# A decode block on one core: w_down loaded with seven following rows per partition, the MLP's inner units in steps of seven

## The chip, the cores and the metric

The kernel runs on one core of one Trainium2 chip. The metric is the device time of one execution in microseconds, lower is better. The core has five engines with a queue each: PE (TensorE, matmuls; PEld are its weight loads), DVE (VectorE), ACT (ScalarE), POOL (GpSimd) and SP (SyncE), which here issues the loads. Sixteen DMA engines move the data.

## The reference, cut to what matters

Four tokens (B = 4, one position each, D = 512) go through two layers, both with the same weights and the same cache: attention over a cache of 4,096 positions with 32 query heads and 8 key/value heads of 128, then an MLP with 1,792 inner units. All inputs are bf16.

```python
x = x + A(layernorm(x), k_cache, v_cache, wq, wo)
x = x + B(layernorm(x), w_gate, w_up, w_down)
x = x + A(layernorm(x), k_cache, v_cache, wq, wo)
x = x + B(layernorm(x), w_gate, w_up, w_down)

def B(x, w_gate, w_up, w_down):      # w_gate, w_up: 512 x 1792; w_down: 1792 x 512
    return (sigmoid(x @ w_gate) * (x @ w_up)) @ w_down
```

The sum over the 1,792 inner units of the last product may be taken in any order, if w_gate's and w_up's columns and w_down's rows are taken in the same one.

## The kernel before

**Data.** Keys and values come in loads of 1 MB (one token, one head: 4,096 x 128 bf16) into 12 slots of the on-chip memory (SBUF, 128 partitions); once the last query projection is done, w_q's place serves as four more. Each partition gets 32 following rows, 8,192 bytes in one run. Part of the cache is kept from layer 1 for layer 2 (KEPT). The weights are loaded once and stay: w_q, w_gate and w_up with two following rows per partition, so that a run is as long as two rows; w_o in runs of 1,024 bytes.

**Order.** It is written out by hand. LOADS is the order of the loads: k and v are cache loads, o, g, u, d pieces of the weights; g, u and d stand behind the first 30 loads. `pump` (L340) issues them on SP, in that order, one after another, and stops where no slot is free; a cache load waits on SP until the slot's last reader on PE is done. PROGRAM is the order of the compute steps on PE, DVE, ACT and POOL, one letter per step; a dot is one step of a token's pass from layer 1 to layer 2. Every engine works through its queue in order, and semaphores keep them in step.

**Attention**, for 32 pairs of heads: k is turned by DVE (L983); scores on PE (L1000; four groups of PSUM partitions side by side, 512 columns each, every second element of the keys); row maximum on DVE (L1018), spread over the partitions by PE (L1023); exponential on ACT (L1043); turned back on PE (L1065), copied by ACT (L1117); times the values on PE (L1163, the values as 128x128 weights, four columns streamed); w_o (L1214) and the addition to x on DVE (L1228).

**The MLP of layer 1** is done per token, in four passes (`pass_steps`, L945) spread over layer 1 and the start of layer 2. In a pass the token's normalised x is the weight of a matmul (one column) and w_gate is streamed: `gate_row` (L795) and `up_row` (L820) cut the 1,792 inner units into seven blocks of 256 columns; block f goes to the group of partitions 32*(f % 4), and blocks f and f + 4 share a matmul of 512 columns. So for each of the four parts of D there are four matmuls side by side (three of 512 columns, one of 256), 16 for gate and 16 for up in a pass. The result lies in four rows, partitions 0, 32, 64 and 96 of 512 columns. ACT takes the tanh that stands for the sigmoid (L815), DVE multiplies (L840). `h_turn` (L847) makes columns of it: four matmuls with 128 of the row's columns as weights and `strips`, four columns of the identity that lie 32 elements apart, as what is streamed. `down` (L916, matmuls L922) uses w_down's rows as weights, 56 matmuls with one column each. Then `ln_a`, `ln_b`, `q_row` (L867, matmuls L873: as gate_row, but with w_q in adjacent columns) and `q_turn` (L905) make the queries of layer 2. When the last pass has its queries, `yield_wq` gives w_q's place to the cache loads.

**The MLP of layer 2** is done for all four tokens at the end, behind the last attention: `gate` (L732, matmuls L737) and `up_half` (L764, matmuls L771) use 128 columns of w_gate or w_up as weights and stream four columns, 56 matmuls each; the last product (L1421) has the hidden units as weights and streams w_down, 56 matmuls of 128 columns.

**The order of the inner units before** comes from w_down's load (wparts, L328): block k of 256 rows gives each partition two following rows, a run of 2,048 bytes. Unit e + 2p of the block is then partition p of column e. So `gate` and `up_half` take every second column of w_gate and w_up as weights, and `h_turn` every second column of the row:

```python
"wd": lambda n: (wd_sb[:, 8 * n:min(8 * n + 8, KF), :].rearrange("p (k e) n -> p k e n", e=2),
                 B_w_down[8 * n * P:min(8 * n + 8, KF) * P, :].rearrange("(k p e) n -> p k e n", p=P, e=2)),
```

with KF = 14 blocks of 128 units, KW = 7 and P = 128. The first of the two loads is 1,024 KB, the second 768 KB.

Of the kernel before, what the change touches and what calls it, by code (L numbers as in the profile page):

```python
# [145 lines left out]
def bass_interleave_layers__gqa_block_cached__glu_gated_glu__decode_kernel(  # L146
# [17 lines left out]
    P = 128  # L164
# [3 lines left out]
    KF = F // P  # L168
# [20 lines left out]
    def sbt(shape, dtype, name):  # L189
        cnt[0] += 1  # L190
        return es.enter_context(nc.sbuf_tensor(f"{name}_{cnt[0]}", list(shape), dtype))

    def pst(name):
        return es.enter_context(nc.psum_tensor(name, [P, 512], dt.float32))
# [5 lines left out]
    wg_sb = sbt([P, KD, F], dt.bfloat16, "wg")  # L200
    wu_sb = sbt([P, KD, F], dt.bfloat16, "wu")
    wd_sb = sbt([P, KF, D], dt.bfloat16, "wd")
# [53 lines left out]
    row_sb = t_bf.rearrange("p (h d) -> p h d", h=2)  # L256
# [19 lines left out]
    M_ps = [pst("M_ps0"), pst("M_ps1")]  # L276
# [36 lines left out]
    def two_rows(sb, n):  # L313
        return sb[:, 2 * n:2 * n + 2, :].rearrange("p e n -> p (e n)")

    def row_pairs(w, n):
        return w[2 * n * P:2 * (n + 1) * P, :].rearrange("(p e) n -> p (e n)", e=2)

    def cols(c):
        return bass.ds(c // 2 * 2 * P + c % 2, P, step=2)  # L320

    KW = KF // 2
# [2 lines left out]
                         A_wo[n * REP * P:(n + 1) * REP * P, :].rearrange("(h p) n -> p h n", p=P)),  # L325
        "wg": lambda n: (two_rows(wg_sb, n), row_pairs(B_w_gate, n)),
        "wu": lambda n: (two_rows(wu_sb, n), row_pairs(B_w_up, n)),
        "wd": lambda n: (wd_sb[:, 8 * n:min(8 * n + 8, KF), :].rearrange("p (k e) n -> p k e n", e=2),  # L328
                         B_w_down[8 * n * P:min(8 * n + 8, KF) * P, :].rearrange("(k p e) n -> p k e n", p=P, e=2)),
    }  # L330
    assert KF == 14
    wkeys = {"wg": ["wg0", "wg1"], "wu": ["wu0", "wu1"], "wd": ["wd0", "wd1"]}
# [36 lines left out]
    def dve(fn, reads=(), writes=()):  # L369
        return S.inst("dve", fn, reads=reads, writes=writes)  # L370

    def act(fn, reads=(), writes=()):
        return S.inst("act", fn, reads=reads, writes=writes)
# [34 lines left out]
    for k in range(KD):  # L408
# [3 lines left out]
                lhsT=x_io[0:Bn, cols(k)],  # L412
                rhs=ident_bf[0:Bn, 0:Bn],
# [62 lines left out]
    def bc(ap2, n, nb):  # L476
        return ap2.unsqueeze(1).broadcast_to([P, n, nb])
# [254 lines left out]
    def gate(fc0, fc1):  # L732
        fns = []
        for fc in range(fc0, fc1):
            for k in range(KD):
                fns.append(
                    (lambda fc, k: lambda e: e.matmul(  # L737
                        M_ps[0][:, 64 + fc * Bn:64 + (fc + 1) * Bn],
                        lhsT=wg_sb[:, k, bass.ds(fc // 2 * 2 * P + fc % 2, P, step=2)],
                        rhs=xc_bf[:, k, 0:Bn],  # L740
                        start=(k == 0),
                        stop=(k == KD - 1),
                    ))(fc, k)
                )
        if fc0 == 0:
            S.group("pe", fns, reads=["xcb"] + wkeys["wg"], writes=["M0"])
            return
        S.last_write["M0"] = S.group("pe", fns, reads=["xcb"] + wkeys["wg"])
        dve(
            lambda e: e.tensor_tensor(  # L750
                gs_sb.rearrange("p (k b) -> p k b", k=KF),
                M_ps[0][:, 64:64 + KF * Bn].rearrange("p (k b) -> p k b", k=KF),
                bc(rs, KF, Bn),
                ALU.mult,
            ),
            reads=["M0", "rs"],
            writes=["ra"],
        )
        act(
            lambda e: e.activation(t_sb, gs_sb, ACTF.Tanh),  # L760
            writes=["ra"],
        )

    def up_half(h):  # L764
        M, mk = ((M_ps[1], "M1"), (O_ps[1], "O1"))[h]
        f0 = KW * h
        fns = []
        for fc in range(f0, f0 + KW):
            for k in range(KD):
                fns.append(  # L770
                    (lambda fc, k: lambda e: e.matmul(  # L771
                        M[:, 64 + fc * Bn:64 + (fc + 1) * Bn],
                        lhsT=wu_sb[:, k, bass.ds(fc // 2 * 2 * P + fc % 2, P, step=2)],
                        rhs=xc_bf[:, k, 0:Bn],
                        start=(k == 0),
                        stop=(k == KD - 1),
                    ))(fc, k)
                )
        S.group("pe", fns, reads=["xcb"] + wkeys["wu"], writes=[mk])
        dve(  # L780
            lambda e: e.scalar_tensor_tensor(
                out=hT_bf[:, f0:f0 + KW, :],
                in0=t_sb.rearrange("p (k b) -> p k b", k=KF)[:, f0:f0 + KW, :],
                scalar=1.0,
                in1=M[:, 64 + f0 * Bn:64 + (f0 + KW) * Bn].rearrange("p (k b) -> p k b", k=KW),
                op0=ALU.add,
                op1=ALU.mult,
            ),
            reads=["ra", mk],
            writes=[("rc", "rd")[h]],  # L790
        )

    strips = ident_bf.rearrange("p (s w) -> p s w", s=4)[:, :, 0]

    def gate_row(part):  # L795
        fns = []
        wv = wg_sb.rearrange("p k (f d) -> p k f d", d=2 * P)
        for k in range(2 * part, 2 * part + 2):
            for st in range(4):
                nt = (KW - st + 3) // 4  # L800
                fns.append(
                    (lambda k, st, nt: lambda e: e.matmul(
                        M_ps[0][32 * st:32 * st + 1, 0:nt * 2 * P],
                        lhsT=xc_bf[:, k, 0:1],
                        rhs=wv[:, k, bass.ds(st, nt, step=4), :],
                        start=(k == 0),
                        stop=(k == KD - 1),
                    ))(k, st, nt)
                )
        if part == 0:  # L810
            S.group("pe", fns, reads=["xcb"] + wkeys["wg"], writes=["M0"])
            return
        S.last_write["M0"] = S.group("pe", fns, reads=["xcb"] + wkeys["wg"])
        act(
            lambda e: e.activation(t_row[:, :], M_ps[0][:, :], ACTF.Tanh, scale=rs[:, 0:1]),  # L815
            reads=["rs", "M0"],
            writes=ROW,
        )

    def up_row(part):  # L820
        fns = []
        wv = wu_sb.rearrange("p k (f d) -> p k f d", d=2 * P)
        for k in range(2 * part, 2 * part + 2):
            for st in range(4):
                nt = (KW - st + 3) // 4
                fns.append(
                    (lambda k, st, nt: lambda e: e.matmul(  # L827
                        M_ps[1][32 * st:32 * st + 1, 0:nt * 2 * P],
                        lhsT=xc_bf[:, k, 0:1],
                        rhs=wv[:, k, bass.ds(st, nt, step=4), :],  # L830
                        start=(k == 0),
                        stop=(k == KD - 1),
                    ))(k, st, nt)
                )
        if part == 0:
            S.group("pe", fns, reads=["xcb"] + wkeys["wu"], writes=["M1"])
            return
        S.last_write["M1"] = S.group("pe", fns, reads=["xcb"] + wkeys["wu"])
        dve(
            lambda e: e.scalar_tensor_tensor(  # L840
                out=row_sb[:, 0, :], in0=t_row[:, :], scalar=1.0, in1=M_ps[1][:, :], op0=ALU.add, op1=ALU.mult
            ),
            reads=["rc", "rd", "rb", "M1"],
            writes=["ra"],
        )

    def h_turn():  # L847
        fns = []
        for t in range(2):
            for e_ in range(2):  # L850
                fns.append(
                    (lambda t, e_: lambda e: e.matmul(
                        M_ps[0][:, bass.ds(8 * t + e_, 4, step=2)],
                        lhsT=row_sb[:, 0, bass.ds(2 * P * t + e_, P, step=2)],
                        rhs=strips,
                        start=True,
                        stop=True,
                    ))(t, e_)
                )
        S.group("pe", fns, reads=["ra"] + IDENT, writes=["M0"])  # L860
        dve(
            lambda e: e.tensor_copy(hT_bf[:, :, 0], M_ps[0][:, 0:KF]),
            reads=["M0"],
            writes=["rc", "rd"],
        )
# [520 lines left out]
    for c in range(KD):  # L1386
        for e_ in range(2):
# [3 lines left out]
                    lhsT=xT[:, c // 2 * 2 + e_, :],  # L1391
                    rhs=ident_w[:, P // 2 * (c % 2):P // 2 * (c % 2 + 1)],
# [19 lines left out]
        writes=["rowk"],  # L1412
    )
    up_half(0)
    up_half(1)
    for part in range(2):
        fns = []
        for k in range(KW * part, KW * part + KW):
            for c in range(KD):
# [3 lines left out]
                        lhsT=hT_bf[:, k, :],  # L1423
                        rhs=wd_sb[:, k, c * P:(c + 1) * P],
# [70 lines left out]
```

## Time and profile before

| | |
|---|---|
| median of 3 runs | 313.84 us (313.71 to 313.90) |
| the profiled execution's own time | 316.34 us |
| its span (first to last instruction) | 314.50 us |
| PE, PEld busy | 227.9 us (72%), 146.8 us (47%) |
| DVE, ACT, POOL busy | 176.3 us (56%), 104.5 us (33%), 40.4 us (13%) |
| read from memory | 119.80 MB, 381 GB/s over the span |
| mean granted TensorE clock | 0.74 |

The profile is one execution; its times are in microseconds from the span's start. A busy time counts an instruction from start to end; matmuls overlap, so the busy time of a group is the time covered, and the mean of one can be far longer than their spacing. The 40 slices of the page are 7.9 us each; a digit is the busy share in tenths. The table of stretches has the busy time and number of instructions of PE, PEld, DVE, ACT and POOL in a stretch, then the granted clock, the share of the DMA engines and what they moved. The chain that ended last goes back from the last instruction, at each step to what released it; it is read here in order of time. For a line or tile there are the minimum, median and maximum duration in ns, and the times of the first and last start.

### The profile page before, as it was taken

Reading aid. Unit: us, or ns where it says so; the run is one execution under the profiler, and the core shown is the slowest. Engines: PE = TensorE matmul, PEld = TensorE weight load, DVE = VectorE, ACT = ScalarE, POOL = GpSimd, SP = SyncE. Lnnn points to the kernel's source line nnn. Section 1 sums busy time; section 2 is a strip of 40 time slices with the busy share of each in tenths; the row PEclk is TensorE's granted clock in tenths of the full one; section 3 lists DMA queues with packets and bytes.
Section 4 is the critical chain, followed back from the end, with each engine's and each line's share of the span. In section 5 each row is a group of like instructions: output and inputs, shape, how many; then the busy total and the mean of one; then the engine's idle time right before and its main releaser. Section 6 shows DMA issues by size and latency. Waiting matters only on the chain.

```text
span 314.5 us, 10670 instructions
## 1 busy us (share of the span) xinstructions
PE 227.9 (72%) x4562; PEld 146.8 (47%) x4562; DVE 176.3 (56%) x399; ACT 104.5 (33%) x347; POOL 40.4 (13%) x205
## 2 busy tenths in 40 slices
PE   1233355425969879987789898977777869799966
PEld 1221043413455355746446847254555543455865
DVE  6267625067324568484942675864675777932243
ACT  2002202600213365343325442434334201556420
POOL 0011111001000214111113011020121011121000
PEclk9999999999999999576855557555555575755555
DMA  7999999999999999999999999999999998999910
GB/s 294 419 397 394 410 404 409 402 420 420 400 416 419 373 394 420 424 418 418 420 391 390 417 349 424 425 419 418 418 418 387 412 373 315 380 426 423 414 51 5
DMA packets 20790, 120.49 MB, mean 383 GB/s; under 512 B 1924, under 2 KB 6024, under 8 KB 7688
## 3 DMA queue, kind: packets, MB, share of 16 engines
q1 hardware_dynamic: 20720, 119.81, 94.1%
q8 instruction: 36, 0.59, 0.7%
q14 instruction: 10, 0.08, 0.1%
q10 hardware_dynamic: 24, 0.01, 0.0%
HBM read 119.80 MB, written 0.00 MB: 381 GB/s over the span
## 4 chain that ended last, share of the span: by engine, by line
PE 36%; DMA 34%; DVE 10%; SPq 9%; ACT 6%; issue 4%; POOL 1%; DVEq 0%; ACTq 0%; POOLq 0%
DMA slot<-in_A_v_cache_dram 17%; DMA slot<-in_A_k_cache_dram 13%; PE O_ps L1163 10%; PE S_ps L1000 10%; SPq L366 7%; DVE slot L983 6%; PE PT L1065 4%; DMA wq<-in_A_v_cache_dram 4%; ACT pT L1117 4%; PE O_ps L1214 3%; PE M_ps L873 2%; PE M_ps L922 1%; DVE small L1018 1%; ACT pe L1043 1%; SPq L346 1%
## 5 line engine op out<-in xcount | busy, mean ns | idle before, releaser
L983 DVE STREAM_TRANSPOSE slot<-slot 128x2048 f32<-128x2048 f32 (+1 forms) x55 | 104.6, 1911 | 18.3 <-DMA slot<-in_A_k_cache_dram 18.2
L1117 ACT ACTIVATE pT<-PT 32x128 bf16<-32x128 f32 x236 | 63.1, 267 | 69.2 <-PE PT L1065 33.3
L1000 PE MATMUL S_ps<-slot,qz 128*16 128x512 bf16 x512 | 59.5, 586 | 25.4 <-DVE slot L983 13.2
L1163 PE MATMUL O_ps<-pT,slot 128*128 128x4 bf16 x1696 | 54.8, 166 | 20.0 <-ACT pT L1117 9.9
L1163 PEld LDWEIGHTS O_ps<-pT,slot 128*128 128x128 bf16 x1696 | 51.1, 104 | 34.8 <-ACT pT L1117 13.1
L1043 ACT ACTIVATE pe<-S_ps,small 128x512 bf16<-128x512 f32 x32 | 22.0, 687 | 68.8 <-DVE small L1032 39.1
L1018 DVE TENSOR_REDUCE small<-S_ps 128x1 bf16<-128x512 f32 x32 | 22.0, 689 | 38.2 <-PE S_ps L1000 33.9
L724 POOL COPY qz<-qs 32x32 bf16<-32x32 bf16 x128 | 26.0, 203 | 128.2 <-PE S_ps L1000 87.0
L1065 PE MATMUL PT<-ident_bf,pe 128*128 128x64 bf16 (+1 forms) x288 | 27.7, 236 | 7.8 <-ACT pe L1043 7.2
L1065 PEld LDWEIGHTS PT<-ident_bf,pe 128*128 128x128 bf16 (+1 forms) x288 | 20.4, 124 | 21.6 <-ACT pe L1043 11.4
L1000 PEld LDWEIGHTS S_ps<-slot,qz 128*16 128x16 bf16 x512 | 10.3, 99 | 40.1 <-DVE slot L983 15.1
L1214 PE MATMUL O_ps<-oT,wo 128*128 128x1 bf16 (+1 forms) x640 | 20.3, 165 | 3.7 <-issue 1.8
L1214 PEld LDWEIGHTS O_ps<-oT,wo 128*128 128x128 bf16 x640 | 18.7, 104 | 6.1 <-issue 2.8
L1076 POOL CAST small<-small 128x1 bf16<-128x1 f32 x32 | 6.0, 186 | 94.7 <-ACT pe L1043 67.7
L1194 DVE TENSOR_TENSOR oT<-O_ps,small 128x8 bf16<-128x8 f32 (+1 forms) x32 | 5.3, 165 | 22.3 <-PE O_ps L1163 15.3
L1032 DVE CUSTOM_DVE_ANT_0 MS<-MS,small 128x64 f32<-128x64 f32 x32 | 9.1, 285 | 10.4 <-PE MS L1023 7.4
L873 PE MATMUL M_ps<-wq,small 128*1 128x512 bf16 x128 | 14.6, 609 | 0.0
L1023 PE MATMUL MS<-valid_p,small 128*128 128x64 bf16 x32 | 7.2, 225 | 6.0 <-DVE small L1018 5.9
L1228 DVE TENSOR_TENSOR small<-small,O_ps 128x4 f32<-128x4 f32 (+1 forms) x21 | 3.1, 150 | 13.1 <-PE O_ps L1214 12.9
L888 ACT ACTIVATE t_row<-M_ps,small 128x512 bf16<-128x512 f32 x4 | 2.7, 687 | 23.0 <-DVE small L1032 11.9
L1023 PEld LDWEIGHTS MS<-valid_p,small 128*128 128x128 bf16 x32 | 3.5, 109 | 13.5 <-DVE small L1018 11.7
L827 PE MATMUL M_ps<-wu,small 128*1 128x512 bf16 (+1 forms) x64 | 8.7, 543 | 0.0
(117 smaller groups left out, 182.9 us busy)
## 6 DMA issues: line engine op xcount, KB each, us to landing
slot<-in_A_v_cache_dram SPq DMA_DIRECT2D x49, 1024.0 KB, 12.0
slot<-in_A_k_cache_dram SPq DMA_DIRECT2D x45, 1024.0 KB, 12.0
wq<-in_A_v_cache_dram SPq DMA_DIRECT2D x6, 1024.0 KB, 12.7
wq<-in_A_wq_dram SPq DMA_DIRECT2D x2, 2048.0 KB, 10.1
wo<-in_A_wo_dram SPq DMA_DIRECT2D x8, 512.0 KB, 16.7
wg<-in_B_w_gate_dram SPq DMA_DIRECT2D x2, 896.0 KB, 17.9
wu<-in_B_w_up_dram SPq DMA_DIRECT2D x2, 896.0 KB, 21.3
wd<-in_B_w_down_dram SPq DMA_DIRECT2D x1, 1024.0 KB, 24.1
```

The costliest lines, as they stand in the source:

```text
L366: "sp", (lambda dst, frm: lambda e: e.dma_start(dst, frm))(dst, frm), sem, writes=[key], deps=deps
L724: (lambda a, ps: lambda e: e.tensor_copy(qz_sb[ps, :, :, a, :], qs_sb[b][ps, :, u * REP:(u + 2) * REP].rearrange("p t (u r) -> p u t r", r ...
L873: (lambda k, st: lambda e: e.matmul(M_ps[h][32 * st:32 * st + 1, :], lhsT=xc_bf[:, k, 0:1], rhs=wv[:, k, h, :, st, :], start=(k == 0), sto ...
L983: dve(lambda e: e.transpose(kf, kf), writes=[f"s{st}"])
L1000: (lambda t, b2, e_, c, r0, ul: lambda e: e.matmul(S_ps[p][r0:r0 + 4 * REP, :], lhsT=qz_sb[:, ul, t, :, :].rearrange("p a r -> p (a r)"), ...
L1018: dve(lambda e: e.tensor_reduce(rm_bf, S_ps[p][:, :], AX.X, ALU.max), reads=[f"S{p}"], writes=["rmb"])
L1023: lambda e: e.matmul(MS[:, 0:16 * REP], lhsT=rm_bf.broadcast_to([P, P]), rhs=valid_p[:, :], start=True, stop=True),
L1043: lambda e: e.activation(pe_sb.rearrange("p j m -> p (j m)"), S_ps[p][:, :], ACTF.Exp, bias=nm_sb, scale=exp_scale, accum_out=sm_sb,),
L1065: (lambda q0, q1, c0, m0, m1, a0, a1: lambda e: e.matmul(PT[q0:q1, c0:c0 + 16 * (a1 - a0)], lhsT=pe_flat[:, m0:m1], rhs=valid_bf[:, :, 4 * ...
L1117: (lambda dst, frm: lambda e: e.activation(dst, frm, ACTF.Copy))(dst, frm),
L1163: (lambda n, x, c, j: lambda e: e.matmul(bank[:, ul * REP:(ul + 1) * REP], lhsT=vv[:, x * JG + c * 4 + j, :], rhs=pT[:, x % 2, j, x // 2, ...
L1214: (lambda c, r: lambda e: e.matmul(out_w[:, c * nb:(c + 1) * nb], lhsT=wo_sb[:, us[0] * REP + r, cols(c)], rhs=oT_sb[:, us[0] * REP + r, c ...
```

## The change

w_down is loaded in two equal parts of 896 rows, seven following rows per partition, 7,168 bytes in one run (128 runs per part for 512 and 384 of 2,048 bytes). Inner unit 896h + 7p + j is now partition p of column 7h + j. So the weights of `gate` and `up_half` are 128 columns of w_gate and w_up in steps of seven (14 bytes), and the streamed operands of `gate_row` and `up_row` are, for each of seven values of j, 2 x 128 columns in steps of seven instead of 256 adjacent ones. The row then holds the units in the order of the partitions, and `h_turn` takes 128 adjacent columns as weights; two of its matmuls stream three columns instead of four, and the results are written adjacent.

```diff
-        "wd": lambda n: (wd_sb[:, 8 * n:min(8 * n + 8, KF), :].rearrange("p (k e) n -> p k e n", e=2),
-                         B_w_down[8 * n * P:min(8 * n + 8, KF) * P, :].rearrange("(k p e) n -> p k e n", p=P, e=2)),
+        "wd": lambda n: (wd_sb[:, KW * n:KW * n + KW, :].rearrange("p k n -> p (k n)"),
+                         B_w_down[KW * P * n:KW * P * (n + 1), :].rearrange("(p k) n -> p (k n)", p=P)),
...
@@ gate (L737); up_half (L771) likewise with wu_sb
-                        lhsT=wg_sb[:, k, bass.ds(fc // 2 * 2 * P + fc % 2, P, step=2)],
+                        lhsT=wg_sb[:, k, bass.ds(fc // KW * KW * P + fc % KW, P, step=KW)],
...
@@ gate_row (L797, L802); up_row likewise with wu_sb
-        wv = wg_sb.rearrange("p k (f d) -> p k f d", d=2 * P)
+        wv = wg_sb.rearrange("p k (h q j) -> p k j h q", h=2, j=KW)
...
-                        rhs=wv[:, k, bass.ds(st, nt, step=4), :],
+                        rhs=wv[:, k, bass.ds(st, nt, step=4), :, :],
...
@@ h_turn (L852)
-                        M_ps[0][:, bass.ds(8 * t + e_, 4, step=2)],
-                        lhsT=row_sb[:, 0, bass.ds(2 * P * t + e_, P, step=2)],
-                        rhs=strips,
+                        M_ps[0][:, KW * e_ + 4 * t:KW * e_ + 4 * t + 4 - t],
+                        lhsT=row_sb[:, 0, P * (2 * t + e_):P * (2 * t + e_ + 1)],
+                        rhs=strips[:, 0:4 - t],
```

More of the change, by code (lines that the diff above doesn't have):

```diff
@@ L772, in up_half @@
                         M[:, 64 + fc * Bn:64 + (fc + 1) * Bn],
-                        lhsT=wu_sb[:, k, bass.ds(fc // 2 * 2 * P + fc % 2, P, step=2)],
+                        lhsT=wu_sb[:, k, bass.ds(fc // KW * KW * P + fc % KW, P, step=KW)],
                         rhs=xc_bf[:, k, 0:Bn],
@@ L821, in up_row @@
         fns = []
-        wv = wu_sb.rearrange("p k (f d) -> p k f d", d=2 * P)
+        wv = wu_sb.rearrange("p k (h q j) -> p k j h q", h=2, j=KW)
         for k in range(2 * part, 2 * part + 2):
@@ L829, in up_row @@
                         lhsT=xc_bf[:, k, 0:1],
-                        rhs=wv[:, k, bass.ds(st, nt, step=4), :],
+                        rhs=wv[:, k, bass.ds(st, nt, step=4), :, :],
                         start=(k == 0),
```

## The prediction

> **What bounds the kernel now.** I first read the strip of 40 slices on the profile's page (7.9 us each).
>
> ```profile
> PE   1233355425969879987789898977777869799966
> DMA  7999999999999999999999999999999998999910
> GB/s 294 419 397 394 410 404 409 402 420 420 400 416 419 373 394 420 424 418 418 420 391 390 417 349 424 425 419 418 418 418 387 412 373 315 380 426 423 414 51 5
> ```
>
> The DMA engines are busy from the first slice to about 300 us; after that the transfers are over and 12 us of a tail are left. So two things set the end: how much DMA time is lost before 300 us, and how long the tail is. The second view is the chain that ended last, in order of time (start, length, what). First the tail:
>
> ```profile
> 307.03 0.30 PE M_ps L737 x8
> 307.39 1.27 PE M_ps L737 x48
> 308.66 0.75 PE M_ps L771 x28
> 309.41 0.75 PE O_ps L771 x28
> 310.16 1.62 PE S_ps L1421 x56
> 311.88 0.35 DVE slot L1434
> ```
>
> PE runs here without a break, from the gate (L737) through up (L771) to down (L1421): a nanosecond more on one of its instructions is a nanosecond at the end. Each of the 56 + 56 gate and up matmuls loads 128x128 weights and streams four columns. They follow each other every 1.27 us / 48 = 26.5 ns, so their weight loads set the pace. For the four per-token MLP passes, the chain again and the table of stretches (PE, PEld, DVE, ACT, POOL, clock, DMA share, GB/s):
>
> ```profile
> 85.77 1.83 PE M_ps L827 x4
> 87.70 0.69 DVE t_row L840
> ...
> 104.00:106.00 2.00, 1.20 (x28) 0.56 (x20) 1.67 (x3) 0.00 (x0) 0.81 (x4) 1.00 0.97 356
> 106.00:108.00 2.00, 1.86 (x32) 0.82 (x29) 0.81 (x4) 1.15 (x3) 0.22 (x2) 1.00 0.91 356
> 108.00:110.00 2.00, 2.00 (x36) 1.02 (x35) 0.34 (x1) 1.47 (x7) 0.48 (x3) 1.00 0.95 373
> ```
>
> Pass 1 lies on the chain: from 66.6 to 128.2 us it holds PE, DVE, ACT and POOL work and no transfer. Behind the pass, at 104 to 110 us, the DMA falls from the 420 GB/s that it reaches at 116 to 160 us to 356: SP waits there for PE to give back slots. A delay of PE in pass 1 is therefore lost DMA time.
>
> **The change part by part.**
>
> 1. The loads of w_down. The instruction lists differ on SP only in these two issues: 128x3584 elements each (7,168 bytes in one run per partition) for 128x4x1024 and 128x3x1024 (2,048-byte runs). The trace's packet records add up to 4.94 us of the 16 engines for the 896 packets of 2,048 bytes, and to 8.87 us for the 512 of 7,168 bytes of w_gate and w_up; 256 such would be 4.43. So up to 0.5 us of DMA time goes away, at about 82 to 89 us. I count it as nothing: 15 us later the queue runs low because slots come late, not because bytes are slow, and a DMA that is 0.5 us ahead waits 0.5 us longer there. Were that stall not there, it would be -0.5. The two issues hold SP's queue for 10.18 us (63.48 to 73.65); the issues of w_gate take 0.42 each, so 9.3 us of SP are freed. The loads behind them stand in the same queue behind a DMA share of 1.02, and SP next waits for PE (83.8 to 94.5): 0.
>
> 2. The turn of the row (L852), 16 matmuls in all: weights adjacent instead of every second column, and two of four read three columns for four. They are spaced by 27 ns as contiguous ones are: 0. DVE, ACT and POOL have the same instructions as before.
>
> 3. The steps of seven. The moving operand of the row passes (L802, L827), so far runs of 256 adjacent columns, and the weights of the tail (L737, L771), so far every second column, are now read 14 bytes apart. No instruction on PE of before reads so, and this price decides all. The nearest rows:
>
> ```profile
> 71.39 0.85 PE O_ps L1214 x32
> 93.58 0.85 PE O_ps L1163 x32
> ...
> L737 PE MATMUL M_ps<-small,wg x56: 166/166/186, 307.0 to 308.5; 128*128 128x4 bf16 x56
> L905 PE MATMUL M_ps<-ident_bf,t_row x32: 167/168/188, 100.3 to 267.5; 128*128 128x4 bf16 x32
> L852 PE MATMUL M_ps<-ident_bf,t_row x16: 168/168/189, 90.4 to 255.7; 128*128 128x4 bf16 x16
> ```
>
> L1214's weights are every second column, L1163's adjacent: both 26.6 ns apart, so a step of 4 bytes is free (L1000 streams with that step as well, 16 in 1.81 to 1.91 us, as L873 does adjacent ones). L905 and L852 stream four columns that lie 64 bytes apart, and last 168 ns where four adjacent ones last 166 at the clock of 0.5 (and 164 at 1.0). That is 2 ns over three further columns, **0.67 ns for each column that lies apart** (1.33 at the full clock). So the step of 14 bytes costs between 0 and 0.67 ns a column at the clock of 0.5 that holds in most of the passes and in the tail. I take 0.67: a step of seven passes over six columns of seven, which is nearer to L905's reads, that use one column of 32, than to L1214's, that use every second. It rests on a difference of 2 ns, which is why the other end keeps a large chance.
>
> The Trainium skill speaks on both sides. "SBUF — State Buffer", Specifications, says that a read needs at least two hits in a 16-byte line for full bandwidth; seven bf16 elements apart there is hardly more than one. By it seven of eight columns would pay, and the sum below would be 0.6 us less.
>
> *Tail.* L873's 128 matmuls (32 groups of four, side by side) are busy 14.6 us: 0.456 us a group, 0.89 ns a column. 0.67 more is a ratio of 1.75. The weight loads are paced by columns too (L1163 and L1214: 128 in 26.6 ns, whatever the four or one columns streamed behind), so I give them the same ratio, and 26.5 ns becomes 46.4: 112 x 19.9 = **+2.2 us**, all of it on the chain. Bounds 0 and 3.0 (a doubling). L1421 reads w_down as before.
>
> *Pass 1.* Gate and up are four groups each, 512 columns at the longest: 4 x 512 x 0.67 = 1.37 us each. Gate ends at 85.2, and the next on PE (L1023) waits until 85.5 for DVE (L1018): 0.3 hidden. Up is on the chain. 2.4 us reach the release of slots. What is queued behind on PE is the exponentials' transposes and scores, and SP waits for these. The dip at 104 to 110 us becomes deeper by most of it: **+2.0**, bounds 0.5 and 2.4.
>
> *Passes 2 to 4.* 2.7 us each again. Pass 2 (134.5 to 137.8) is followed by idle times of PE of 0.54, 0.68 and 0.52, the last for a DMA at 142.4, and at 147.7 by 12 us of the chain on a transfer: absorbed. Pass 3 is followed by 0.66 idle for a DMA at 189.8, then by chain work on PE up to 225, over which the DMA is never dry: mostly absorbed. Pass 4 is followed by 0.85 (DMA, 254.8) and 1.80 (DVE behind a DMA, 259.6): 2.65 of 2.7, but its up runs partly at the full clock, where a column pays 1.33, +0.7. I take **+0.6** for all three, bounds 0 and 3.
>
> Sum: 2.2 + 2.0 + 0.6 = +4.8. The profiled execution (316.34 us, span 314.50) would come to 321.1. The runs without profile have a median of 313.84, 2.5 less; the difference carries over, **318.6 us**. With all low or all high bounds of this case (tail 1.4 to 3.0) it is 315.7 to 322.2.
>
> **The rivals.**
>
> *A, not slower: the step of seven is free.* Place: the read of weights and columns; price 0 a column. For it: the step of two costs nothing (26.6 against 26.6 ns), and 14 bytes is much nearer to 4 than to 64; 2 ns of L905 is little. Against: these are the only rows with wide steps, L905 and L852 agree, and at the clock of 1.0 the gap is 4 ns. Then only the DMA's gain is left, 0 to 0.5 us: 313.3 to 313.8, and I would say 313.7. It decides when the price is under about 0.15 ns a column: the tail then costs under 0.5 us, pass 1 is within what its 0.3 us of idle time and the DMA's gain cover. "SBUF — State Buffer", Door 1, says in the box on lines also that one may stride freely by 8 bf16 elements, which this step keeps to; the trace has no row for that.
>
> *B, far slower: the four streams hinder each other,* as four columns or four parts of a weight load are then read from many places at once. If a load of 128 columns went at one column per 0.89 ns, it would take 114 ns: the tail alone + 112 x 87 = 9.8 us (323.6); groups of four times 0.456 us make each pass 11 us longer, and with pass 1 alone it is 334 or more. For it: these loads do go four times faster than one column per 0.89 ns, so parts of them are read side by side. Against: L1000's four streams with their step of two show no loss.
>
> *C: only one of the two reads pays.* Tail alone +2.2 (316.0), passes alone +2.6 (316.4). For it: weights and moving columns are read by separate instructions that overlap (PE and PEld). Against: both are paced by columns.
>
> That the change does not do what it says is out: the two issues and the operand steps are in the instruction lists.
>
> **How the numbers follow.** Forecast case 0.48; A 0.40; B 0.07; C 0.05. This kernel's runs (313.71 to 313.90) can tell apart about 0.2%, 0.6 us. Of A, 0.32 is within that and 0.08 is faster by more (the 0.5 us saved plus transfers that fall better). Faster 0.08, same 0.32, slower 0.60. The range goes from 313.2, A with nearly all its gain, to 322.2, the upper bound of the forecast; B and a part of A's fast end are left out. The forecast's own range is 315.7 to 322.2.
>
> **What would show it.** In the tail, L737's 48 matmuls: 2.2 us for 1.27 if right, 1.27 in A, 5 and more in B. A group of four in L802 and L827: 0.80 us for 0.456. At 104 to 110 us, a DMA share well under 0.91. The issues of w_down at about 0.43 us each and 256 packets of 7,168 bytes more. The forecast is wrong if the tail keeps its length from 307.0 to 311.9, or if the passes are longer and the DMA nevertheless ends at the same time.

## The result and the profile after

The changed kernel takes **324.67 us** (median of 5 runs, 324.07 to 325.28) against 313.78 for the kernel before (5 runs, 313.19 to 313.90): a ratio of 1.0352, 95% interval 1.0334 to 1.0369, or +10.9 us. The forecast was +4.8, with a range up to 322.2: the direction was right, the size forecast was less than half of the measured one. The profiled execution of after took 324.99 us, its span is 323.2, the mean granted clock 0.69.

The strip of 40 slices of after (8.1 us each):

```profile
DMA  7999999999999899999999999999998989999700
GB/s 293 423 396 395 410 405 406 405 421 417 421 415 339 309 410 418 423 419 385 422 368 399 405 389 375 411 359 426 419 420 335 420 313 357 421 423 420 316 4 3
```

The transfers end at 306.4 us, 8 us later than in the second profile of before (298.35, experiment 1), although there are no more bytes (119.80 MB in both). The digits hardly show it; the row of GB/s does, with 339 and 309 behind pass 1 and further values under 400 in the twenties and thirties of the row. Less than a third of the loss is in the tail. This is its chain in after, in order of time:

```profile
312.70 0.52 PE M_ps L737 x8
313.28 2.55 PE M_ps L737 x48
315.83 1.49 PE M_ps L771 x28
317.32 1.49 PE O_ps L771 x28
318.82 1.62 PE S_ps L1421 x56
```

Against the chain of before, gate has grown by 0.22 and 1.28 us and up by twice 0.74: 2.98 in all. L1421 has stayed at 1.62. The weights are now 53.3 ns apart instead of 26.5, so each load costs twice as much as before.

The row matmuls of pass 1 in PE's timeline of after (start, length, instructions):

```profile
83.42 3.31 PE L802 MATMUL M_ps<-wg,small 128*1 128x512 bf16 x16
86.83 3.31 PE L827 MATMUL M_ps<-wu,small 128*1 128x512 bf16 x16
```

Before, both took 1.87 us, so this pass has 2.9 us more of PE. A group of four is 780 ns behind the last, where it was 420. The stretches behind pass 1 (columns as in the prediction):

```profile
106.00:108.00 2.00, 1.19 (x21) 0.27 (x12) 1.67 (x3) 0.00 (x0) 0.81 (x4) 0.50 0.63 209
108.00:110.00 2.00, 1.86 (x39) 0.85 (x36) 1.09 (x4) 0.86 (x3) 0.02 (x1) 0.50 0.73 258
```

The dip that was 0.91 and 356 GB/s at its lowest is now 0.63 and 209.

To see where the 11 us come in, I compare the start of each instruction in after with that of the same one in a second profile of before (experiment 1 below; span 312.0, so 11.2 us shorter). The lag, by which after is later, grows by these steps:

| part | lag added, us | forecast, us |
|---|---|---|
| up to pass 1 | 0.3 | 0 |
| pass 1 | 2.7 | 2.0 |
| pass 2 | 1.2 | 0.6 for passes 2 to 4 |
| pass 3 | 3.0 | |
| pass 4 | 1.0 | |
| tail | 3.0 | 2.2 |

So every term was too small, but one was wrong by a factor: passes 2 to 4 add 5.2 us where the forecast has 0.6. The experiments ask whether these are really the passes' prices, whether the load of w_down has a share, and why pass 3 is not absorbed.

My theory: the price of the reads is about as forecast, the load is worth nothing, and each pass's longer time on PE gives slots back late, so that transfer time is lost at once, even where the DMA row of the strip shows no gap. The rivals: the new load of w_down costs something itself; the lags are the chance of single executions; or the reads with wide steps disturb the transfers directly, beyond the PE time that they take.

### The profile page after: what moved, and what is told of

It reads as the page before. It is cut to its first block, busy times and chain, and to the rows that moved or that the text cites. A ratio compares the mean times of both kernels' runs of the same rounds, so it can differ in the third digit from the quotient of the medians.

```text
span 323.2 us, 10670 instructions
## 1 busy us (share of the span) xinstructions
PE 241.2 (75%) x4562; PEld 148.5 (46%) x4562; DVE 175.4 (54%) x399; ACT 104.7 (32%) x347; POOL 40.5 (13%) x205
## 3 DMA queue, kind: packets, MB, share of 16 engines
HBM read 119.80 MB, written 0.00 MB: 371 GB/s over the span
## 4 chain that ended last, share of the span: by engine, by line
PE 47%; DVE 17%; DMA 15%; SPq 7%; issue 5%; ACT 5%; another core or an unknown queue 2%; POOL 1%; DVEq 0%; ACTq 0%; POOLq 0%
DMA slot<-in_A_k_cache_dram 15%; PE S_ps L1000 12%; PE O_ps L1163 11%; DVE slot L983 11%; PE PT L1065 5%; SPq L366 5%; PE O_ps L1214 4%; PE M_ps L873 3%; ACT pT L1117 3%; SPq L346 2%; PE M_ps L827 2%; DVE small L1018 2%; PE M_ps L802 2%; PE M_ps L922 1%
## 5 line engine op out<-in xcount | busy, mean ns | idle before, releaser
L1000 PE MATMUL S_ps<-slot,qz 128*16 128x512 bf16 x512 | 61.4, 589 | 25.3 <-DVE slot L983 12.4
L1163 PE MATMUL O_ps<-pT,slot 128*128 128x4 bf16 x1696 | 54.2, 166 | 16.3 <-ACT pT L1117 9.0
L1163 PEld LDWEIGHTS O_ps<-pT,slot 128*128 128x128 bf16 x1696 | 50.8, 104 | 31.9 <-issue 13.7
L827 PE MATMUL M_ps<-wu,small 128*1 128x512 bf16 (+1 forms) x64 | 16.7, 864 | 0.0
L1032 DVE CUSTOM_DVE_ANT_0 MS<-MS,small 128x64 f32<-128x64 f32 x32 | 9.1, 284 | 10.8 <-PE MS L1023 7.0
L802 PE MATMUL M_ps<-wg,small 128*1 128x512 bf16 (+1 forms) x64 | 13.3, 864 | 0.0
```

The source lines that it names most:

```text
L802: (lambda k, st, nt: lambda e: e.matmul(M_ps[0][32 * st:32 * st + 1, 0:nt * 2 * P], lhsT=xc_bf[:, k, 0:1], rhs=wv[:, k, bass.ds(st, nt, st ...
L827: (lambda k, st, nt: lambda e: e.matmul(M_ps[1][32 * st:32 * st + 1, 0:nt * 2 * P], lhsT=xc_bf[:, k, 0:1], rhs=wv[:, k, bass.ds(st, nt, st ...
L1000: (lambda t, b2, e_, c, r0, ul: lambda e: e.matmul(S_ps[p][r0:r0 + 4 * REP, :], lhsT=qz_sb[:, ul, t, :, :].rearrange("p a r -> p (a r)"), ...
L1163: (lambda n, x, c, j: lambda e: e.matmul(bank[:, ul * REP:(ul + 1) * REP], lhsT=vv[:, x * JG + c * 4 + j, :], rhs=pT[:, x % 2, j, x // 2, ...
```

## The experiments

All times are medians with the kernel before run beside them on the same chip; a difference is the ratio less one, times 314 us. The ratio is not that of the two medians, so the plain difference of medians can be some tenths away: 2.8 in place of 2.2 for pass 1, 2.5 in place of 2.9 for the tail.

### 1. The parts of the change, one at a time

The kernel before, run again without any edit:

> The kernel before, unchanged, for a second profile. The changed kernel's profiled execution is 8.65 us longer than the profiled one of before, the medians differ by 10.9. Theory 1: the first profile of before caught a long execution, by some 2.2 us; this one's span is then about 312 (own time 313.8), and it has less lost DMA time than the first profile's, of which about 2.2 us stood at 240 to 264 us. Rival: profiling itself costs this kernel 2.5 us and the changed one nothing; the span is again 314.5.

Measured: 313.68 us (12 runs; ratio 0.9998, 0.9969 to 1.0026). Its profiled execution took 313.8 us, with a span of 312.0. The first profile of before (316.34, span 314.5) was thus a long execution: own time less span is 1.8 us in both, and single executions spread from 311.95 to 315.80.

Only the load of w_down:

```diff
-        "wd": lambda n: (wd_sb[:, 8 * n:min(8 * n + 8, KF), :].rearrange("p (k e) n -> p k e n", e=2),
-                         B_w_down[8 * n * P:min(8 * n + 8, KF) * P, :].rearrange("(k p e) n -> p k e n", p=P, e=2)),
+        "wd": lambda n: (wd_sb[:, KW * n:KW * n + KW, :].rearrange("p k n -> p (k n)"),
+                         B_w_down[KW * P * n:KW * P * (n + 1), :].rearrange("(p k) n -> p (k n)", p=P)),
```

> Only w_down's load of the change (seven rows per partition); gate, up and the turn keep the order of two, so hidden units meet the wrong rows of w_down and the output is not the reference's; no operand shape or step differs from before. Theory 1: the load saves 0.5 us of DMA time that is lost again, ratio 1.000, 313.2 to 313.8. Rival: the load itself disturbs the queue (SP is free 9 us earlier and other loads are issued earlier): +1 us or more, which would explain a part of the 10.9.

Measured: 314.50 us, ratio 1.0011 (0.9978 to 1.0043). The load gives nothing and costs nothing that can be seen; the interval runs from -0.7 to +1.4 us.

Only the weights of the tail:

```diff
@@ gate (L737); up_half (L771) likewise
-                        lhsT=wg_sb[:, k, bass.ds(fc // 2 * 2 * P + fc % 2, P, step=2)],
+                        lhsT=wg_sb[:, k, bass.ds(fc // KW * KW * P + fc % KW, P, step=KW)],
```

> Only the weights of the last gate and up in steps of seven (hidden units in the wrong order, output not the reference's). Theory 1: weight loads 53.3 ns apart for 26.5, 112 x 26.8 = +3.0 us, all at the end: 316.8. Rival: DVE's chain hides a part of gate, +1.5 to 2.5.

Measured: 316.35 us, ratio 1.0092 (1.0062 to 1.0122), +2.9 us. The chain of this kernel has the same tail as after:

```profile
304.42 2.55 PE M_ps L737 x48
306.97 1.49 PE M_ps L771 x28
308.46 1.49 PE O_ps L771 x28
```

Only the streamed columns of the passes:

```diff
@@ gate_row (L797, L802); up_row likewise
-        wv = wg_sb.rearrange("p k (f d) -> p k f d", d=2 * P)
+        wv = wg_sb.rearrange("p k (h q j) -> p k j h q", h=2, j=KW)
...
-                        rhs=wv[:, k, bass.ds(st, nt, step=4), :],
+                        rhs=wv[:, k, bass.ds(st, nt, step=4), :, :],
```

> Only the streamed operands of the four passes in steps of seven (hidden units in the wrong order, output not the reference's). Theory 1, all but the tail is from here: +7.9 us, 321.7. As I predicted the passes: +2.6 to 3.2 at the doubled price, 316.4 to 317.0; the rest of the 10.9 would then be the load's or come from both together.

Measured: 321.40 us, ratio 1.0244 (1.0204 to 1.0284), +7.6 us. The three parts add up to 0.3 + 2.9 + 7.6 = 10.8, and the whole change costs 10.9. By its interval the load can hold 1.4 us at the most, so the first rival does not make the loss: the passes are 70% of it. Nearly nothing is left for the turn of the row, which was not run by itself.

### 2. One pass at a time

The same edit as in the last experiment, for one of the four passes alone (APART names them, counted from 0; here pass 1):

```diff
+    PASS = []
+    APART = (0,)
...
+        apart = PASS.index(b0) in APART
+        wv = wg_sb.rearrange("p k (h q j) -> p k j h q", h=2, j=KW) if apart else wg_sb.rearrange("p k (f d) -> p k f d", d=2 * P)
...
+    PASS.extend(sorted(range(Bn), key=lambda b: last[0, b]))
```

> Steps of seven in the streamed operands of pass 1 alone (hidden units of one token in the wrong order, output not the reference's). All four passes together cost 7.6 us in the run with rows only. Theory 1: a pass is paid where it leaves the transfer queue short, and every pass does; by the lag of the changed kernel behind the second profile of before, pass 1 costs +2.8. Rival, as I predicted: passes 2 to 4 are absorbed, so pass 1 must hold nearly all, +6 or more, by pushing everything after it.

> The same in pass 2 alone. Theory 1: +1.2 by the lag (it grows from 3.0 to 4.2 us there), less if the queue that pass 1 no longer shortens absorbs it: 0 to 1.2. Rival (absorbed): 0.

> The same in pass 3 alone. Theory 1: +2.8 by the lag (4.5 to 7.3 us). Rival (absorbed, as I predicted): 0 to 0.5.

> The same in pass 4 alone. Theory 1: +1.0 by the lag (7.3 to 8.3 us). Rival (absorbed): 0 to 0.3. If the four singles add up to about 7.6 the passes are paid one by one; if to much less, the delay of one makes the next dearer.

and later passes 2 to 4 together, APART = (1, 2, 3):

> Columns in steps of seven in gate_row and up_row of passes 2 to 4 only; pass 1, the tail and the w_down load are as before, so the hidden units of three tokens are out of order and the output is not the reference's. The prediction's own step gave these three passes 0.6 us together. Theory 1 (each pass's longer matmuls run the DMA engines short, pass 3 is not absorbed, and the losses add): between the sum of the single runs, 0.6 + 2.2 + 0.7 = 3.5 us, and what is left of the 7.6 us of all four after pass 1's 2.2, 5.4 us. A value near 3.5 says that the single prices add, one near 5.4 that one pass makes the next dearer; a value under 1.5 would say that pass 3 alone was a stray measurement and the prediction's step stands.

| wide columns in | median, us | ratio (95%) | difference, us |
|---|---|---|---|
| pass 1 | 316.75 | 1.0070 (1.0044 to 1.0095) | +2.2 |
| pass 2 | 315.17 | 1.0020 (0.9991 to 1.0049) | +0.6 |
| pass 3 | 316.20 | 1.0070 (1.0040 to 1.0100) | +2.2 |
| pass 4 | 314.85 | 1.0023 (0.9997 to 1.0050) | +0.7 |
| passes 2 to 4 | 319.39 | 1.0162 (1.0130 to 1.0195) | +5.1 |
| all four | 321.40 | 1.0244 (1.0204 to 1.0284) | +7.6 |

Pass 3 costs as much as pass 1, by runs that do not depend on one execution; that ends the rival of chance. Passes 2 and 4 alone lie close to what can't be told from nothing. Passes 2 to 4 together cost 5.1 us (4.1 to 6.1), and with pass 1's 2.2 they are 7.3 of the 7.6. Their single prices sum to 3.5, but each of these is uncertain by about 0.9 us, and by plain medians the sum is 4.3 against 4.9 together. So it is not shown that one delay makes the next dearer. The bound of 3 us that the forecast gave to these three passes was too low in any case.

### 3. Why pass 3 is not absorbed

These are long stretches of after, and then the same of the second profile of before: after pass 1, pass 2, pass 3 and pass 4.

```profile
96.00:132.00 36.00, 32.27 (x603) 18.47 (x601) 23.00 (x50) 15.21 (x50) 6.63 (x33) 0.50 0.95 373
144.00:180.00 36.00, 31.89 (x701) 21.41 (x702) 19.70 (x50) 13.69 (x47) 6.21 (x31) 0.61 1.00 397
180.00:216.00 36.00, 33.57 (x564) 17.92 (x562) 24.54 (x52) 12.64 (x41) 5.25 (x26) 0.64 0.99 384
240.00:276.00 36.00, 29.24 (x482) 16.53 (x479) 24.90 (x54) 10.72 (x34) 4.86 (x24) 0.64 0.92 362
```

```profile
96.00:132.00 36.00, 32.12 (x636) 19.57 (x633) 22.30 (x46) 17.97 (x60) 6.43 (x32) 0.50 1.01 411
144.00:180.00 36.00, 30.67 (x637) 20.87 (x641) 21.58 (x47) 14.10 (x48) 6.23 (x31) 0.55 1.01 413
180.00:216.00 36.00, 32.16 (x570) 17.98 (x562) 22.96 (x52) 14.25 (x47) 5.28 (x26) 0.59 1.00 412
240.00:276.00 36.00, 30.39 (x526) 18.02 (x522) 27.79 (x55) 11.11 (x35) 6.09 (x30) 0.59 0.97 380
```

The windows are the same in time, although after is some us behind in its work by then. The last two columns are to be read together. At 180 to 216 us the share falls only from 1.00 to 0.99, which looks as if nothing had happened; but 384 for 412 GB/s over 36 us is 28 x 36 = 1,008 KB, or 2.4 us at the 415 GB/s of an undisturbed stretch. In the same way the stretch behind pass 1 loses 3.3 us, that behind pass 2 1.4, that behind pass 4 1.6. The sum is 8.7 us, and the transfers end 8.06 us later (298.35 and 306.41). The profile counts a DMA engine as busy as long as it has a packet, and the packets take longer: the median packet of 8,192 bytes takes 309 ns, and above that the packets of after lose 11.2 us per engine against 7.7 before. So of the 8.06 us slower packets make 3.5, the new packets of w_down save 0.5, and some 5.1 are time in which a part of the 16 engines had no packet; once the transfers run, there is no moment at which none of the 16 has one. Behind pass 3 it is mostly the packets: at 180 to 216 us their mean is 335 ns for 317, which is 1.9 of the 2.4 us. The long ones follow a gap in SP's issues: from 190 to 196 us of after, while the queue runs down, their mean is still 312 ns, and at 198 to 203 it is 372, with some packets of up to 1.6 us. Why they take longer there, no run shows.

That SP's issues come late can be read from its timeline (start, length, what). These are the two loads between which pass 3 lies, in the second profile of before, in after, with wide columns in pass 3 alone, and in the kernel with more time on PE that follows below:

```profile
183.74 5.66 SPq L366 DMA_DIRECT2D slot<-in_A_k_cache_dram  x2
188.25 8.23 SPq L366 DMA_DIRECT2D slot<-in_A_k_cache_dram  x2
183.88 8.26 SPq L366 DMA_DIRECT2D slot<-in_A_k_cache_dram  x2
187.42 7.68 SPq L366 DMA_DIRECT2D slot<-in_A_k_cache_dram  x2
```

An issue itself takes 0.33 us. So the second load is issued 5.3 us behind the first one in before, and 7.9, 7.9 and 7.4 us in the others. SP waits for PE to be done with a slot: at 180 to 212 us its longest wait for PE's L1163 is 4.9 us in before and 7.5 in after.

With wide columns in pass 2 alone the issue there is held as much longer (8.6 us for 6.3), and that kernel costs 0.6 us: how late an issue is does not by itself say what is lost.

The kernel with wide columns in pass 3 alone, at the stretches of pass 2 and pass 3:

```profile
144.00:180.00 36.00, 30.45 (x633) 20.80 (x633) 21.34 (x45) 13.83 (x47) 6.19 (x31) 0.55 1.00 411
180.00:216.00 36.00, 32.42 (x529) 16.36 (x527) 23.30 (x54) 12.91 (x42) 5.23 (x26) 0.64 0.98 396
```

Ahead of the changed pass the rate is that of before; in its stretch it falls by 16 GB/s, 1.4 us. The loss follows the edit.

It remains whether it comes from the time on PE or from the wide reads as such. While the reads of pass 1 and 2 run in after (83 to 91 and 137 to 144 us), the DMA moves 421 and 417 GB/s; the rate falls behind them. While those of pass 3 run (188 to 195 us) it moves 389, but the second profile of before has 367 in its pass 3 too (183 to 187), without a wide read. As a test, the next kernel adds time to PE without a wide read: 28 further matmuls of 512 or 256 adjacent columns in each pass, whose results are overwritten.

```diff
@@ gate_row; up_row likewise with 4 for 3
+        if part == 0:
+            for r in range(3):
+                for st in range(4):
+                    nt = (KW - st + 3) // 4
+                    fns.append(
+                        (lambda r, st, nt: lambda e: e.matmul(
+                            M_ps[0][32 * st:32 * st + 1, 0:nt * 2 * P],
+                            lhsT=xc_bf[:, r, 0:1],
+                            rhs=wv[:, r, bass.ds(st, nt, step=4), :],
...
```

> Before, with 28 more matmuls in each pass that read adjacent columns and are overwritten (three more groups of four in gate, four more in up): 7 x 0.43 = 3.0 us of PE more per pass, which is what steps of seven add (2.9 to 3.2), without a wide read. Theory 1, only PE's time counts: as rows alone, +7.6 us (6.5 to 8.5). Rival, the wide reads themselves slow the transfers (the changed kernel's 8 KB packets took 3.1 us of the sixteen engines more): clearly less, +4 or below.

Measured: 318.04 us, ratio 1.0143 (1.0103 to 1.0183), +4.5 us (3.2 to 5.7). That is less than theory 1 said, and the interval holds the rival's +4. Its stretch behind pass 3:

```profile
180.00:216.00 36.00, 31.88 (x568) 18.36 (x568) 24.82 (x56) 13.06 (x43) 5.24 (x26) 0.59 0.98 378
```

378 GB/s without a single wide read: time on PE alone is enough for this loss. For the size, the traces give a reason: the added groups ran partly at the full clock (213 ns each in place of 420), so that they added about 1.5, 2.1, 2.3 and 3.5 us to the passes, 9.4 in all, where the step of seven adds 3.1, 2.9, 2.9 and 4.4, 13.3 in all (both against the second profile of before, gate and up each from first start to last end). Per microsecond of PE that is 0.48 (0.34 to 0.61) against 7.6 / 13.3 = 0.57 (0.48 to 0.67). These agree within their intervals, though the PE times are of one execution each; a small direct effect of the wide reads beside it is not excluded.

### 4. The price by the step

One kernel whose tail weights and pass columns use a different step in each group, 1 to 16 elements. The spacing is read from its trace.

> The price of the step by itself: in the tail, weights of gate and up in steps of 1, 2, 3, 4, 5, 6, 7, 8, 9, 12 and 14 (eight to sixteen loads each, each step on a line of its own); in the passes gate and up with steps 4 and 5, 6 and 8, 14 and 16, 3 and 7. The output is not the reference's, since hidden units stand in another order and some columns are read twice. Theory 1, two reads must fall into one 16-byte line: up to step 4 spaced 26.5 ns and groups of four 0.45 us, from step 5 on dearer, 53.3 ns at 7 and not more beyond. Rival, free below 16 bytes: it can't hold at 7; then a rise with every step, 2.0 at 7 and 4 at 14.

The time (321.84 us, one execution) says nothing here, as all steps are mixed. The streamed columns, from the table of groups: each line of that kernel is one step. L155 has step 3, then 4, 5, 6, 7, 8, and L182 has 16; the first line is L802 of before, with adjacent columns (busy time, mean ns of one):

```profile
L802 PE MATMUL M_ps<-wg,small 128*1 128x512 bf16 x48 | 7.5, 620 | 0.0
L155 PE MATMUL M_ps<-wg,small 128*1 128x512 bf16 x12 | 1.9, 604 | 0.0
L158 PE MATMUL M_ps<-wg,small 128*1 128x512 bf16 x12 | 2.0, 628 | 0.0
L161 PE MATMUL M_ps<-wu,small 128*1 128x512 bf16 x12 | 2.4, 737 | 0.0
L164 PE MATMUL M_ps<-wg,small 128*1 128x512 bf16 x12 | 2.9, 848 | 0.0
L167 PE MATMUL M_ps<-wu,small 128*1 128x512 bf16 x12 | 3.3, 966 | 0.0
L170 PE MATMUL M_ps<-wu,small 128*1 128x512 bf16 x12 | 3.8, 1078 | 0.0
L182 PE MATMUL M_ps<-wu,small 128*1 128x512 bf16 x12 | 3.9, 1097 | 0.0
```

Up to a step of 4 (8 bytes) nearly nothing is to be paid, then 112 ns for each further element, and from 8 (16 bytes) on it is flat. The spacing of the last groups of four goes the same way: 423 ns at step 3, 465, 557, 666, 780, 901 at 8, 929 at 14. The weight loads of the tail do so too, by their spacing: 26.9 ns up to step 3, 33.5 at 4, 40.0, 46.6, 53.3 at 7, 61 at 8, 59 to 60 at 9, 12 and 14: 6.67 ns an element. So theory 1 was right that the price begins behind step 4 for streamed columns and stops rising, but it stops at 8 and not at 7. The rival, a rise up to 14, is out.

The Trainium skill ("SBUF — State Buffer", Specifications) asks for two hits in each line of 16 bytes for the full bandwidth. The rise from a step of 8 bytes up to one of 16, and none beyond, agrees with it. So does the shape of the rise: counted out, with steps of 5, 6, 7 and 8 a quarter, a half, three quarters and all of the columns stand alone in their 16 bytes, and the means above (737, 848, 966 and 1,078 from 628 at step 4) have gone 0.24, 0.49, 0.75 and all of the way. (The prediction counted seven of eight columns for the step of seven; it is six.) It does not explain that weight loads pay 6.6 ns at a step of 4 already. Door 1 of the same page of the Trainium skill says that 8 bf16 elements may be strided freely; here that step makes the longest weight loads, 61 ns for 26.9, and the measurement decides.

### 5. A smaller step

If a step of 4 is nearly free, w_down could be loaded with four following rows (4,096 bytes in one run), the tail with steps of four (of two for the last two blocks), and the passes with adjacent columns again. The turn of the row then takes six matmuls for four (not shown in the diff):

```diff
+    def units(fc):
+        n = 4 if fc < 12 else 2
+        return bass.ds(fc // 4 * 4 * P + fc % 4, P, step=n)
...
-                        lhsT=wg_sb[:, k, bass.ds(fc // 2 * 2 * P + fc % 2, P, step=2)],
+                        lhsT=wg_sb[:, k, units(fc)],
...
-                        rhs=wv[:, k, bass.ds(st, nt, step=4), :],
+                        rhs=wv[:, k, 4 * P * st:4 * P * st + 2 * P * nt],
```

> w_down with four following rows per partition (4,096-byte runs) for twelve of the 14 blocks and two for the last two; gate and up of the passes read adjacent columns, one group of 512 units per strip; the tail's weights in steps of four. Theory 1: weights in steps of four are free, 0.4 us of DMA time are saved and mostly lost again: 313.4 to 313.9, ratio 0.998 to 1.000. Rival, a step of four costs too: +1.5 to 3 us in the tail.

Measured: 316.34 us, ratio 1.0082 (1.0054 to 1.0110), +2.6. Of the 112 weight loads 96 have the step of four, and they explain 96 x 6.6 ns = 0.6 of it. The row matmuls last no longer than before (1.87 us), and yet this execution is 2.2 us behind the second profile of before at 212 us, 1.1 at 242 and 2.0 at 290. I did not find where these 2 us come from; it stays open. As the load alone gave nothing that could be seen (experiment 1), I see no reason to expect a gain from another order of the rows; none further was run.

## Why the prediction was right and wrong, point by point

- **What bounds the kernel** (DMA time lost before 300 us, and the tail): right. Of the 11.2 us between the profiles, 8.06 are a later end of the transfers and 3.0 are tail.
- **The load of w_down**, counted 0: nothing speaks against it (+0.3, interval -0.7 to +1.4). The saving in DMA time is there, 4.4 us for the 256 packets of 7,168 bytes against 4.94, and goes under. The two issues were thought to take 0.43 us each; they take 1.4 and 2.1 (1.6 and 8.5 before); why they are not as short as those of w_gate was not tested:

```profile
L346 SPq DMA_DIRECT2D wd<-in_B_w_down_dram x2: 1416/1768/2119, 63.6 to 65.1; - x2
```

- **The turn of the row**, counted 0: nothing speaks against it; its matmuls last 167 ns (168 before), and the three other parts make up the whole change.
- **The price of a column**, 0.67 ns at the clock of 0.5, for streamed columns: right, (780 - 420) / 512 = 0.70. That it doubles at the full clock was wrong in form: a group takes 780 ns at either clock, so against the 213 ns of the full clock the price is 1.1 ns a column. That 0.67 fits was luck: neither of the two rows that the choice rested on (a step of 4 bytes and one of 64) lies in the range where the price changes, and where it is flat again, at a step of 14 elements, a column costs (929 - 420) / 512 = 0.99.
- **The tail**, +2.2: measured +2.9, and +2.98 in the chain. The weight loads were given the ratio of the streamed columns, 1.75; they double, 26.5 to 53.3 ns, the upper bound of the text.
- **Pass 1**, +2.0: measured +2.2 alone, 2.7 in the whole change. The mechanism (late slots, a deeper dip at 104 to 110 us) is the one seen.
- **Passes 2 to 4**, "+0.6 for all three, bounds 0 and 3": this is the step that failed. Measured: +5.1. What failed in it is the sentence on pass 3, "chain work on PE up to 225, over which the DMA is never dry: mostly absorbed". Pass 3 costs 2.2 us by itself and 3.0 behind the delays of passes 1 and 2. The working had PE on the chain there and did not follow what that means for SP: the next load is issued 7.9 us behind the last instead of 5.3. The test, a DMA that runs dry, was the wrong one: with a share of 0.99 to 1.00 the engines already moved 384 to 397 GB/s instead of 412. The text's allowance for passes 2 and 4 (nothing and 0.7) lies within what they cost as single edits (0.6 and 0.7, both not clear of nothing).
- **"The difference carries over"**, 2.5 us from the profiled execution to the median: right for the sum, as after was measured against the median too. But it was the spread of executions that the profile had caught, not a price of profiling.
- **The rivals.** A, a free step, is out: the price is there in every trace. B, streams that hinder each other, is out: groups of four take 780 ns, not the four times 456 ns that B asks for. C, only one read pays, is out: tail and passes pay, 2.9 and 7.6.
- **The range** ended at 322.2, 2.5 under the measured time. Its upper end took 3 us for the three passes; with the 5.1 measured it would have been 324.3, so this one term makes most of the miss.

## What to carry to other kernels

Where PE's progress gives back the buffers that loads wait for, a delay on PE can be lost transfer time although the DMA row shows no gap; here 3 to 4 us more on PE in one pass cost 2.2 in two of the four passes and about 0.6 in the others. Read GB/s beside the DMA share, and look for stretches below the best rate, not for empty ones. Elements of bf16 that PE reads, streamed or as weights, could here lie up to three apart at no cost, and four apart at a tenth more for streamed columns and a quarter more for weights; at seven apart weight loads took twice as long, and groups of streamed columns 1.9 times as long at the clock of 0.5. Before a layout is changed for longer runs in a load, ask what the load is worth: here it was 0.5 us of DMA time that was not on the path, against 112 weight loads that were.

## What the runs showed of the hardware that was not expected

- The price of a step has three parts: free up to 3 elements and small at 4, a straight line up to 8, and flat from there to 16. At step 7, groups of four take about 780 ns at the granted clock of 0.5 (137 to 141 us of after) and at 1.0 (191 to 194 us): there the pace did not follow PE's clock.
- Packets of 8,192 bytes take longer behind a gap in the issues, and the engines count as busy meanwhile: shares of 0.98 to 1.00 went with 378 to 397 GB/s where an undisturbed stretch has 412 and more.
- Twelve executions of the kernel before spread by 4 us (311.95 to 315.80, experiment 1). So a single profile can lie 2.5 us off the median, as the first one of before did.
